# Moving three groups of loads in GpSimd's queue of a fused retention and SwiGLU kernel

## The chip, the cores and the metric

The kernel runs on one core of a Trainium2 chip. The metric is the device time of one execution in microseconds; the time of a kernel is the median of its runs, and lower is better. Where the text says PE, DVE, ACT, POOL and SP it means TensorE, VectorE, ScalarE, GpSimd and SyncE. PEld is the weight load of PE. "POOL's queue" is the in-order list of instructions that GpSimd's sequencer works through; a DMA that is issued from it takes its place among GpSimd's arithmetic.

## What is computed

A retention recurrence over 4 batches, 8 heads, 768 steps of 64 channels, and behind it an RMS norm and a SwiGLU feed-forward layer over the 3072 rows that come out:

```
gamma = 1.0 - 2.0 ** (-5.0 - arange(H))
for t in range(S):
    state = gamma * state + outer(k[:, :, t], v[:, :, t])
    y[:, :, t] = scale * q[:, :, t] @ state
x   = y as (B * S, H * D)
xn  = x / sqrt(mean(x * x) + 1e-6) * rms_g
out = (silu(xn @ w_gate) * (xn @ w_val)) @ w_out
```

All inputs and the output are float32. x has 512 columns, the hidden layer 1536.

## The kernel before

**Tiling.** The 768 steps are cut into six chunks of 128. Inside a chunk the recurrence is done in matrix form: scores q k-transposed under a causal mask with decay, times v, plus q times the state of the chunks before; the state is advanced by k-transposed times v, with v decayed first (`vp`). A chunk has 4 batches. Chunks 0 and 1 take them two at a time, in "pairs" (tiles `q2b`, `k2b`, `v2f`, whose partitions 0 to 63 hold one batch and 64 to 127 the other, two steps to a partition). Chunks 2 to 5 take them one at a time, in "units" (tiles `qb`, `kb`, `v_f`).

**Transposes.** Scores need q and k with channels on partitions. In chunks 0 and 1 PE transposes them (`tp`, L233) and DVE or ACT copies the result out of PSUM. From chunk 2 on the DMA engines transpose them: `t_dma` (L449 to L453) issues two DMA transposes, q first, from SP's queue, each waiting for the load of its source tile. SP's queue also carries the stores of the output (`store`, L545 and L547), and is in order.

**The feed-forward part.** `gv` (L521) makes 128 or 256 columns of the gate product and of the value product on PE (L533), silu on ACT (L537) and their product on DVE (`hT`, L538). `down` (L549) multiplies by w_out (L552), copies out of PSUM on ACT (L554) and stores. The feed-forward part of one chunk is interleaved by hand with the recurrence of the next one, so that PE has work.

**Order.** The program is scheduled by hand: each engine's queue holds its instructions in the order in which the Python code emits them, and nothing moves them afterwards. POOL's queue has both arithmetic and nearly all loads. What stands in it, in order, at the three places that matter here:

- At the start: q and k of pair (0,0) (two DMAs each, one a batch), the iotas `off` and `offp` (L133, L135), q and k of pair (0,1), the iotas `pos_p` and `pos_n` (L139, L141), two small products (L194), four loads of gate and value weights (`load_w`, L86), v of pair (0,1). The two halves of the first v, pair (0,0), are not in it: SP issues them. The first (L119) goes at once; the second (L570) has a dependency, made by hand, on DVE's `late` (L166), so that SP holds it back until then.
- In chunk 0's second half: `power(0, 1)` (L346, the reciprocal root of the mean square), then q, k and v of pair (1,0) (two DMAs each), then `vp_pair(0, 1)` (L276, the decayed v, which `kvp(0, 1)` on PE, L305, waits for), then two loads of weights. Later `vp_pair(1, 0)` reads the v just loaded.
- Between chunk 0's last products and chunk 1's output: `state_diag(1)` (L321), the six loads of units (2,0) and (2,1) (`load`, L105; three DMAs each), `rstd(1, 0)` (L430, then L346), `state_cast(0)` (L324), `vp_pair(1, 1)`, then the six loads of units (2,2) and (2,3). `rstd(1, 0)` waits for ACT's squares of chunk 1's output (L425).

After them SP transposes: `t_dma(2, 0)`, `t_dma(2, 1)`, then the store of `down(0, 3)`, then `t_dma(2, 2)`, `t_dma(2, 3)`. The first PE instructions that need the transposes are `a_pair(2, 0)` (L461, eight matmuls for unit (2,0), eight for unit (2,1)), in step 5 of chunk 1's feed-forward steps; those of units (2,2) and (2,3) are needed by `a_pair(2, 1)` in step 10.

At the start, `v_cast(0)` (ACT, L271) turns v of pair (0,0) to bf16 as `vb`, and `y0(0, 0)` (PE, L291) multiplies by it. `v_cast(1)` does the same for pair (0,1); on ACT it stands ahead of the silu of `gv(0, 2, 3)` and `gv(0, 3, 4)`. `heat` (L215) gives PE matmuls whose result nobody reads.

Of the kernel before, what the change touches and what calls it, by code (L numbers as in the profile page):

```python
# [12 lines left out]
ALU = mybir.AluOpType  # L13
# [3 lines left out]
def kernel(  # L17
# [11 lines left out]
    nc = tc.nc  # L29
# [15 lines left out]
    work = ctx.enter_context(tc.tile_pool(name="work", bufs=4))  # L45
    psum = ctx.enter_context(tc.tile_pool(name="psum", bufs=1, space=bass.MemoryType.PSUM))

    SYNC_DEP = mybir.DependencyInfo(mybir.DependencyClass.Sync, mybir.DependencyReason.DATA)

    srcs = dict(q=q, k=k, v=v)  # L50

    unit_v = {n: s.rearrange("b h (c p) d -> c b p h d", p=C) for n, s in srcs.items()}
# [1 line left out]
    pair_v = {n: s.rearrange("b h (c j e) d -> c b j h (e d)", c=NCH, e=2) for n, s in srcs.items()}  # L54
# [6 lines left out]
    order = [1, 7, 5, 6, 3, 4, 2, 0]  # L61
# [21 lines left out]
    def load_w(n0, n1, *kinds):  # L83
        sl = slice(n0 * 128, n1 * 128)
        for i in kinds or (0, 1):
            nc.gpsimd.dma_start(out=(wg_b, wv_b)[i][:, :, sl], in_=(wg_v, wv_v)[i][:, :, sl])  # L86
# [3 lines left out]

    U = {}

    def load_pair(c, p, n, batches=(0, 1), after=None, eng=None):
        u = U.setdefault((c, p), {})
        if n not in u:
            if n == "v":
                u[n] = work.tile([128, H, 2 * D], F32, name="v2f", bufs=3)
            else:
                u[n] = work.tile([128, H, 2 * D], BF16, name=n + "2b", bufs=4)
        for b in batches:  # L100
            i = (eng or nc.gpsimd).dma_start(out=u[n][b * 64:b * 64 + 64], in_=pair_v[n][c, 2 * p + b])  # L101
            if after is not None:
                tc.add_manual_dep(i.ins, after.ins.name, SYNC_DEP, reason="transfer order")

    def load(c, b, names="qkv"):  # L105
        u = U.setdefault((c, b), {})
        for n in names:
            if n == "v":
                x = work.tile([128, H, D], F32, name="v_f", tag="v_f", bufs=6)
                nc.gpsimd.dma_start(out=x, in_=unit_v[n][c, b])  # L110
            else:
                x = work.tile([128, DM], BF16, name=n + "b", bufs=8)
                nc.gpsimd.dma_start(out=x.rearrange("p (h d) -> p h d", h=H), in_=unit_v[n][c, b])  # L113
            u[n] = x
# [18 lines left out]
    nc.gpsimd.iota(off, pattern=[[1, 128]], base=0, channel_multiplier=-1)  # L133
    for i in range(2):
        nc.gpsimd.iota(offp[i * 64:i * 64 + 64], pattern=[[-1, 2], [1, 2], [2, 64]], base=0, channel_multiplier=-2)  # L135
    load_pair(0, 1, "q")
    load_pair(0, 1, "k")
    for i in range(2):
# [24 lines left out]

    late = const.tile([128, 256], F32, name="late")
    offp_f = offp.rearrange("p e f j -> p (e f j)")
    late_i = nc.vector.tensor_scalar(out=late, in0=offp_f, scalar1=0.0, scalar2=1.0e7, op0=ALU.is_lt, op1=ALU.mult)  # L166
    reach = const.tile([128, 256], F32, name="reach")
    nc.vector.tensor_tensor(out=reach, in0=offp_f, in1=late, op=ALU.add)
    causal_p = const.tile([128, 256], BF16, name="causal_p")
# [84 lines left out]
                        nc.tensor.matmul(ps[i][t, o:o + 128], kt[r, x, b, e], qt[r, x, b], start=True, stop=True)  # L254
        u["a_ps", a] = ps

    last_mask = [None]

    def ap_mask(c, p, a, i):
        u = U[c, p]  # L260
        am = work.tile([128, 2, 2, 128], BF16, name="am2", tag="am", bufs=12)
        m = mask0[a][i] if c == 0 else causal_p[:, None, :].to_broadcast([128, 2, 256])
        last_mask[0] = nc.vector.tensor_tensor(
            out=am.rearrange("p x e t -> p x (e t)"),
            in0=u["a_ps", a][i].rearrange("p (x t) -> p x t", x=2), in1=m, op=ALU.mult)
        u["am", a, i] = am
# [6 lines left out]
    def vp_pair(c, p):  # L273
        u = U[c, p]
        x = work.tile([128, H * 2, D], BF16, name="vp2", bufs=3)
        nc.gpsimd.tensor_tensor(  # L276
            out=x, in0=u["v"].rearrange("p h (e d) -> p (h e) d", e=2),
            in1=vd_p[:, c].rearrange("p h e -> p (h e)")[:, :, None].to_broadcast([128, 2 * H, D]), op=ALU.mult)
        u["vp"] = x.rearrange("p (h e) d -> p h (e d)", e=2)
# [38 lines left out]
    def state_diag(p):  # L318
        for i in range(2):
            r = slice(i * 64, i * 64 + 64)  # L320
            nc.gpsimd.tensor_copy(st_d[p][r, :, :, i * D:i * D + D], st_f[p][r])  # L321

    def state_cast(p):
        nc.gpsimd.tensor_copy(st_b[p], st_f[p])  # L324
# [18 lines left out]
    def power(c, p):  # L343
        u = pair(c, p)
        r = work.tile([128, 2], F32, name="rstd", bufs=4)
        nc.gpsimd.tensor_tensor(out=r, in0=u["ms"], in1=mhalf, op=ALU.pow)  # L346
        u["rstd"] = r
# [11 lines left out]
    def begin(c):  # L359
        XT[c] = work.tile([128, KS, GT], BF16, name="xnT", bufs=2)  # L360
# [18 lines left out]
    def y1(p):  # L379
        u = U[1, p]  # L380
        u["y"] = [bank("y_ps") for _ in range(2)]
        for b in range(2):
            for hp in range(NHP):
                nc.tensor.matmul(u["y"][b][:, hp * 128:(hp + 1) * 128],
                                 u["qT", hp // 2][:, hp % 2, b].rearrange("p e j -> p (e j)"), st_d[p][:, b, hp],
                                 start=hp == 0, stop=False, skip_group_check=True)
        for h in range(H):
            hp, i = h // 2, h % 2
            for e in range(2):
                for b in range(2):  # L390
                    r = slice(b * 64, b * 64 + 64)
                    nc.tensor.matmul(u["y"][b][:, h * D:h * D + D], u["am", hp // 2, i][r, hp % 2, e, :],
                                     u["vp"][r, h, e * D:e * D + D], start=False,
                                     stop=h == H - 1 and e == 1, skip_group_check=True)
# [11 lines left out]
    def pair(c, p):  # L406
        return U[c, p] if c < 2 else U[c, p, "pair"]
# [25 lines left out]
    def norm(c, p, *units):  # L433
        u = pair(c, p)
        if 0 in units:
            u["xn"] = [work.tile([128, DM], BF16, name="xn", bufs=6) for _ in range(2)]
        for b in units:
            nc.vector.scalar_tensor_tensor(out=u["xn"][b], in0=u["x"][:, b], scalar=u["rstd"][:, b:b + 1], in1=g_bc,  # L438
                                           op0=ALU.mult, op1=ALU.mult)
# [81 lines left out]
    def gv(c, n0, n1, t0, t1):  # L521

        if c not in HT:
            HT[c] = work.tile([128, NFF, GT], BF16, name="hT", bufs=1)
        w = t1 - t0
        m = (n1 - n0) * w
        ps = []
        for wt, name in ((wg_b, "g_ps"), (wv_b, "v_ps")):
            x = bank(name, ffn=True)
            for n in range(n0, n1):  # L530
                o = (n - n0) * w
                for s in range(KS):
                    nc.tensor.matmul(x[:, o:o + w], wt[:, s, n * 128:(n + 1) * 128], XT[c][:, s, t0:t1],  # L533
                                     start=s == 0, stop=s == KS - 1)
            ps.append(x)
        sg = work.tile([128, 512], BF16, name="sg", bufs=4)
        nc.scalar.activation(sg[:, :m], ps[0][:, :m], AF.Silu)  # L537
        return nc.vector.tensor_tensor(  # L538
            out=HT[c][:, n0:n1, t0:t1], in0=sg[:, :m].rearrange("p (n t) -> p n t", t=w),
            in1=ps[1][:, :m].rearrange("p (n t) -> p n t", t=w), op=ALU.mult)  # L540
# [8 lines left out]
    def down(c, b):  # L549
        ps = bank("o_ps", ffn=True)  # L550
        for n in range(NFF):
            nc.tensor.matmul(ps, HT[c][:, n, b * C:(b + 1) * C], wo_b[:, n, :], start=n == 0, stop=n == NFF - 1)  # L552
        o_sb = work.tile([128, DM], F32, name="o_sb", bufs=3)
        nc.scalar.copy(o_sb, ps)  # L554
        store(nc.sync, c, b, slice(0, DM), o_sb)
# [11 lines left out]


    begin(0)
    load_pair(0, 0, "v", (1,), after=late_i, eng=nc.sync)  # L570
    load_w(0, 2)
    load_w(2, 4)
    load_pair(0, 1, "v")
# [59 lines left out]
    squares0(1)  # L633
    eps0(1)
    power(0, 1)
    for n in "qkv":
        load_pair(1, 0, n)
    vp_pair(0, 1)
    load_w(10, 12)
    gv(0, 4, 5, 0, 256)  # L640
    gv(0, 5, 6, 0, 256)
# [19 lines left out]
        load_pair(1, 1, n)  # L661
    gv(0, 6, 7, 256, 512)
    state_diag(1)
    load(2, 0)
    gv(0, 7, 8, 0, GT)
    gv(0, 8, 9, 0, GT)
    for n, e in (("q", "a"), ("k", "v")):
# [12 lines left out]
    state1(0)  # L680
    gv(0, 11, 12, 0, GT)
    y1(0)
    load(2, 1)
    down(0, 0)
    y1_out(0)
    square(1, 0, 0)
# [1 line left out]
    rstd(1, 0)  # L688
    state_cast(0)
    norm(1, 0, 0, 1)  # L690
    vp_pair(1, 1)
    load(2, 2)
    down(0, 1)
# [24 lines left out]
    def L(f, *a):  # L718
        return lambda: f(*a)
# [26 lines left out]
    for c in range(2, NCH):  # L746
# [6 lines left out]
        after = {}  # L753
        if d < NCH:
            after = {
                0: [L(begin, d)],
                1: [L(values, d, 0), L(vp, d, 2), L(vp, d, 3)],
                2: [L(y_out, d, 0, 0)] + [L(load, d + 1, 0)] * more,
                3: [L(y_out, d, 0, 1)] + [L(state_add, d, 0)] * more,
                4: [L(square, d, 0, 0)] + [L(load, d + 1, 1)] * more,  # L760
                5: [L(a_pair, d, 1), L(a_mask, d, 2, 0), L(square, d, 0, 1), L(rstd, d, 0)]
                   + [L(state_cast, 0)] * more,
                6: [L(a_mask, d, 2, 1), L(norm, d, 0, 0), L(x_dma, d, 0, 0)]
# [40 lines left out]
```

## Time and profile before

| | |
|---|---|
| median of 5 runs | 241.34 us |
| the five runs | 240.63 to 242.53 us |
| the profiled execution, its own time | 242.53 us |
| the profiled execution, its span | 240.8 us |
| mean granted PE clock in it | 0.989 |
| PE busy | 228.6 us (95%) |
| DVE, ACT, POOL busy | 129.2, 87.4, 116.8 us |
| moved by DMA | 30.24 MB |

The span runs from the first to the last instruction; 1.7 us of the execution's time lie around it. In the views of the profile a line begins with its start in us from the span's start, then how long it took, then the engine, the line of the code and what was written from what; `x2` says that two instructions are merged. Brackets at the end hold the idle time of that engine just before, and after `<-` what ended it. POOLq or SPq lines are DMA issues. The profiled execution is the slowest of the five.

### The profile page before, as it was taken

What the parts mean: (1) busy time and instruction counts of PE and PEld (TensorE: products, weight loads), DVE (VectorE), ACT (ScalarE), POOL (GpSimd) and SP (SyncE); (2) the same over time, 40 slices, a digit from 0 to 9 for tenths busy, and PEclk for the clock granted to TensorE, in tenths of its full rate; (3) what the DMA queues carried; (4) which work ended last, traced back from release to release, by engine and by line L of the source; (5) the groups of instructions that cost most, each with busy time, mean ns of one, the idle gap of its engine ahead of it and who ended that gap; (6) DMA issues with size and microseconds to landing.
All of it is one profiled execution on the core that took longest, in us unless ns stands there. A gap on an engine that the chain in (4) does not pass through costs nothing.

```text
span 240.8 us, 5437 instructions
## 1 busy us (share of the span) xinstructions
PE 228.6 (95%) x2223; PEld 138.7 (58%) x2223; DVE 129.2 (54%) x222; ACT 87.4 (36%) x176; POOL 116.8 (49%) x151
## 2 busy tenths in 40 slices
PE   7689999999996999999999999999999999999993
PEld 2357784545895875585454585454684444854442
DVE  3756734829492687827866336866345842243300
ACT  2576544132342243235223225323225241323220
POOL 8949699789389821990945901927001000000000
PEclk9979999999999999999999999999999999999998
DMA  8999999999999999999699994994520204200022
GB/s 99 170 205 184 170 181 179 188 204 223 148 109 121 183 145 203 126 141 188 52 147 181 121 156 140 99 185 112 143 77 0 44 3 136 82 3 0 0 87 88
DMA packets 82858, 30.24 MB, mean 126 GB/s; under 512 B 69521, under 2 KB 78481, under 8 KB 82834
## 3 DMA queue, kind: packets, MB, share of 16 engines
q0 software_dynamic: 51408, 16.78, 64.7%
q1 hardware_dynamic: 30752, 12.98, 30.4%
q8 instruction: 17, 0.28, 0.5%
q10 hardware_dynamic: 674, 0.14, 0.3%
q14 instruction: 7, 0.06, 0.1%
HBM read 28.32 MB, written 6.29 MB: 144 GB/s over the span
## 4 chain that ended last, share of the span: by engine, by line
PE 77%; DMA 10%; POOL 7%; DVE 3%; issue 1%; ACT 1%; DVEq 0%; POOLq 0%; ACTq 0%
PE o_ps L552 25%; PE g_ps L533 22%; PE v_ps L533 21%; DMA kT<-kb 6%; DMA v2f<-in_v_dram 4%; PE y_ps L506 2%; POOL q2b L101 2%; PE a_ps L461 2%; POOL k2b L101 2%; PE y_ps L490 1%; PE o_ps L563 1%; PE kv_ps L499 1%; POOL v2f L101 1%; PE t_ps L233 1%; POOL vp L276 1%
## 5 line engine op out<-in xcount | busy, mean ns | idle before, releaser
L538 DVE TENSOR_TENSOR hT<-sg,v_ps 128x512 bf16<-128x512 bf16 (+1 forms) x76 | 49.7, 657 | 75.5 <-PE v_ps L533 71.7
L533 PE MATMUL g_ps<-xnT,wg_b 128*128 128x256 bf16 (+1 forms) x428 | 75.0, 310 | 0.2 <-ACT xnT L221 0.2
L533 PE MATMUL v_ps<-xnT,wv_b 128*128 128x256 bf16 (+1 forms) x428 | 74.9, 309 | 0.0
L537 ACT ACTIVATE sg<-g_ps 128x512 bf16<-128x512 f32 (+1 forms) x76 | 43.4, 574 | 82.8 <-PE g_ps L533 82.8
L552 PE MATMUL o_ps<-wo_b,hT 128*128 128x512 bf16 x276 | 61.4, 379 | 0.0
L533 PEld LDWEIGHTS <-wv_b 128*128 128x128 bf16 x428 | 41.8, 98 | 20.8 <-DMA wv_b<-in_moe_w_val_dram 0.2
L533 PEld LDWEIGHTS <-wg_b 128*128 128x128 bf16 x428 | 40.4, 98 | 20.0 <-issue 0.7
L552 PEld LDWEIGHTS <-hT 128*128 128x128 bf16 x276 | 26.5, 98 | 31.4
L430 POOL TENSOR_SCALAR m<-ms 128x2 f32<-128x2 f32 x10 | 2.2, 219 | 69.7 <-ACT xsq L425 69.7
L554 ACT COPY o_sb<-o_ps 128x512 f32<-128x512 f32 x23 | 13.4, 582 | 43.7 <-PE o_ps L552 43.7
L438 DVE SCALAR_TENSOR_TENSOR xn<-x,rstd,g_bc 128x512 bf16<-128x512 f32 x20 | 21.9, 1120 | 12.8 <-POOL rstd L346 12.8
L470 DVE TENSOR_TENSOR am<-a_ps,causal 128x512 bf16<-128x512 f32 x32 | 20.8, 678 | 0.0
L444 POOL TENSOR_TENSOR vp<-v_f,vd_n 128x512 bf16<-128x512 f32 x16 | 20.1, 1277 | 0.0
L425 ACT ACTIVATE xsq<-x 128x512 bf16<-128x512 f32 x20 | 12.4, 623 | 7.7 <-DVE x L416 7.7
L113 POOL DMA_DIRECT2D kb<-in_k_dram x16 | 14.3, 894 | 1.8 <-DMA wo_b<-in_moe_w_out_dram 1.6
L110 POOL DMA_DIRECT2D v_f<-in_v_dram x16 | 14.7, 916 | 0.9 <-DMA qb<-in_q_dram 0.9
L113 POOL DMA_DIRECT2D qb<-in_q_dram x16 | 15.0, 939 | 0.0
L416 DVE TENSOR_TENSOR x<-y_ps,yd_n 128x512 f32<-128x512 f32 x16 | 10.8, 683 | 0.6 <-PE y_ps L506 0.6
L218 PE MATMUL hot<-ones 128*128 128x512 bf16 x25 | 9.6, 513 | 1.4 <-DVE ones L145 1.4
L276 POOL TENSOR_TENSOR vp<-v2f,vd_p 128x1024 bf16<-128x1024 f32 x4 | 8.2, 2042 | 0.1
L461 PE MATMUL a_ps<-qT,kT 64*128 64x128 bf16 x128 | 5.5, 218 | 2.5 <-DMA kT<-kb 2.1
L346 POOL TENSOR_TENSOR rstd<-m,mhalf 128x2 f32<-128x2 f32 x10 | 7.2, 718 | 0.8
(92 smaller groups left out, 158.0 us busy)
## 6 DMA issues: line engine op xcount, KB each, us to landing
v_f<-in_v_dram POOLq DMA_DIRECT2D x16, 256.0 KB, 8.2
out_dram<-o_sb SPq DMA_DIRECT2D x15, 256.0 KB, 2.3
out_dram<-o_sb SPq DMA_DIRECT2D x17, 128.0 KB, 5.6
qb<-in_q_dram POOLq DMA_DIRECT2D x16, 128.0 KB, 8.0
kb<-in_k_dram POOLq DMA_DIRECT2D x16, 128.0 KB, 7.9
wg_b<-in_moe_w_gate_dram POOLq DMA_DIRECT2D x6, 256.0 KB, 6.2
wv_b<-in_moe_w_val_dram POOLq DMA_DIRECT2D x6, 256.0 KB, 6.8
v2f<-in_v_dram POOLq DMA_DIRECT2D x6, 256.0 KB, 9.4
```

Source lines behind the costliest of these rows:

```text
L101: i = (eng or nc.gpsimd).dma_start(out=u[n][b * 64:b * 64 + 64], in_=pair_v[n][c, 2 * p + b])
L110: nc.gpsimd.dma_start(out=x, in_=unit_v[n][c, b])
L113: nc.gpsimd.dma_start(out=x.rearrange("p (h d) -> p h d", h=H), in_=unit_v[n][c, b])
L425: nc.scalar.activation(xsq, u["x"][:, b], AF.Square, scale=1.0 / math.sqrt(DM), accum_out=u["ms_"][:, b:b + 1])
L438: nc.vector.scalar_tensor_tensor(out=u["xn"][b], in0=u["x"][:, b], scalar=u["rstd"][:, b:b + 1], in1=g_bc, op0=ALU.mult, op1=ALU.mult)
L444: nc.gpsimd.tensor_tensor(out=x, in0=U[c, b]["v"], in1=vd_n[:, c, :, None].to_broadcast([128, H, D]), op=ALU.mult)
L470: nc.vector.tensor_tensor(out=x, in0=u["a_ps"][i].rearrange("p (a t) -> p a t", a=NHP), in1=causal[:, None, :].to_broadcast([128, NHP, 128 ...
L533: nc.tensor.matmul(x[:, o:o + w], wt[:, s, n * 128:(n + 1) * 128], XT[c][:, s, t0:t1], start=s == 0, stop=s == KS - 1)
L537: nc.scalar.activation(sg[:, :m], ps[0][:, :m], AF.Silu)
L538: return nc.vector.tensor_tensor(out=HT[c][:, n0:n1, t0:t1], in0=sg[:, :m].rearrange("p (n t) -> p n t", t=w), in1=ps[1][:, :m].rearrange( ...
L552: nc.tensor.matmul(ps, HT[c][:, n, b * C:(b + 1) * C], wo_b[:, n, :], start=n == 0, stop=n == NFF - 1)
L554: nc.scalar.copy(o_sb, ps)
```

## The change

Three things move, all in or into POOL's queue, and the hand-made dependency and the variable that goes with it are taken out.

1. The second half of the first v (batch 1 of pair (0,0)) is issued from POOL, between `offp` and q of pair (0,1), and no longer from SP behind `late`.
2. v of pair (1,0) is issued after `vp_pair(0, 1)` and no longer before it.
3. The six loads of units (2,0) and (2,1) are issued after `rstd(1, 0)`, `state_cast(0)` and `norm(1, 0, 0, 1)` (the last is on DVE), right ahead of `vp_pair(1, 1)`, and no longer ahead of `rstd(1, 0)`.

The arithmetic, the tiles and their buffer counts stay as they are, and so does the order on PE, ACT and DVE.

```
-    def load_pair(c, p, n, batches=(0, 1), after=None, eng=None):
+    def load_pair(c, p, n, batches=(0, 1), eng=None):
...
-            i = (eng or nc.gpsimd).dma_start(out=u[n][b * 64:b * 64 + 64], in_=pair_v[n][c, 2 * p + b])
-            if after is not None:
-                tc.add_manual_dep(i.ins, after.ins.name, SYNC_DEP, reason="transfer order")
+            (eng or nc.gpsimd).dma_start(out=u[n][b * 64:b * 64 + 64], in_=pair_v[n][c, 2 * p + b])
...
         nc.gpsimd.iota(offp[i * 64:i * 64 + 64], pattern=[[-1, 2], [1, 2], [2, 64]], base=0, channel_multiplier=-2)
+    load_pair(0, 0, "v", (1,))
     load_pair(0, 1, "q")
     load_pair(0, 1, "k")
...
     begin(0)
-    load_pair(0, 0, "v", (1,), after=late_i, eng=nc.sync)
     load_w(0, 2)
...
     power(0, 1)
-    for n in "qkv":
+    for n in "qk":
         load_pair(1, 0, n)
     vp_pair(0, 1)
+    load_pair(1, 0, "v")
     load_w(10, 12)
...
     state_diag(1)
-    load(2, 0)
     gv(0, 7, 8, 0, GT)
...
     y1(0)
-    load(2, 1)
     down(0, 0)
...
     norm(1, 0, 0, 1)
+    load(2, 0)
+    load(2, 1)
     vp_pair(1, 1)
     load(2, 2)
```

More of the change, by code (lines that the diff above doesn't have):

```diff
@@ L46 @@
     psum = ctx.enter_context(tc.tile_pool(name="psum", bufs=1, space=bass.MemoryType.PSUM))
-    SYNC_DEP = mybir.DependencyInfo(mybir.DependencyClass.Sync, mybir.DependencyReason.DATA)
     srcs = dict(q=q, k=k, v=v)
@@ L91, with load_pair @@
     U = {}
-    def load_pair(c, p, n, batches=(0, 1), after=None, eng=None):
+    def load_pair(c, p, n, batches=(0, 1), eng=None):
         u = U.setdefault((c, p), {})
@@ L100, in load_pair @@
         for b in batches:
-            i = (eng or nc.gpsimd).dma_start(out=u[n][b * 64:b * 64 + 64], in_=pair_v[n][c, 2 * p + b])
-            if after is not None:
-                tc.add_manual_dep(i.ins, after.ins.name, SYNC_DEP, reason="transfer order")
+            (eng or nc.gpsimd).dma_start(out=u[n][b * 64:b * 64 + 64], in_=pair_v[n][c, 2 * p + b])
     def load(c, b, names="qkv"):
@@ L135 @@
         nc.gpsimd.iota(offp[i * 64:i * 64 + 64], pattern=[[-1, 2], [1, 2], [2, 64]], base=0, channel_multiplier=-2)
+    load_pair(0, 0, "v", (1,))
     load_pair(0, 1, "q")
@@ L165 @@
     offp_f = offp.rearrange("p e f j -> p (e f j)")
-    late_i = nc.vector.tensor_scalar(out=late, in0=offp_f, scalar1=0.0, scalar2=1.0e7, op0=ALU.is_lt, op1=ALU.mult)
+    nc.vector.tensor_scalar(out=late, in0=offp_f, scalar1=0.0, scalar2=1.0e7, op0=ALU.is_lt, op1=ALU.mult)
     reach = const.tile([128, 256], F32, name="reach")
@@ L255, in ap @@
         u["a_ps", a] = ps
-    last_mask = [None]
     def ap_mask(c, p, a, i):
@@ L262, in ap_mask @@
         m = mask0[a][i] if c == 0 else causal_p[:, None, :].to_broadcast([128, 2, 256])
-        last_mask[0] = nc.vector.tensor_tensor(
+        nc.vector.tensor_tensor(
             out=am.rearrange("p x e t -> p x (e t)"),
@@ L569 @@
     begin(0)
-    load_pair(0, 0, "v", (1,), after=late_i, eng=nc.sync)
     load_w(0, 2)
@@ L635 @@
     power(0, 1)
-    for n in "qkv":
+    for n in "qk":
         load_pair(1, 0, n)
     vp_pair(0, 1)
+    load_pair(1, 0, "v")
     load_w(10, 12)
@@ L663 @@
     state_diag(1)
-    load(2, 0)
     gv(0, 7, 8, 0, GT)
@@ L682 @@
     y1(0)
-    load(2, 1)
     down(0, 0)
@@ L690 @@
     norm(1, 0, 0, 1)
+    load(2, 0)
+    load(2, 1)
     vp_pair(1, 1)
```

## The prediction

> **What bounds the kernel now.** I read the page's totals and slices first, then the chain that ended last, then who waited for whom, then the timeline engine by engine round each place that the diff touches.
>
> ```profile
> PE 228.6 (95%) x2223; PEld 138.7 (58%) x2223; DVE 129.2 (54%) x222; ACT 87.4 (36%) x176; POOL 116.8 (49%) x151
> PE   7689999999996999999999999999999999999993
> DMA  8999999999999999999699994994520204200022
> ```
>
> PE is the bound: after the first 30 us (five slices of 6 us) only slice 13 of its row falls under 9. The DMA row is at 9 for nearly all of the first half: loads there queue. So the end can move only through PE's few gaps. The chain and the waits name them:
>
> ```profile
> 12.67 9.78 DMA v2f<-in_v_dram
> 22.53 1.05 ACT vb L271
> ...
> 62.10 13.80 DMA kT<-kb
> 75.95 0.40 PE a_ps L461 x8
> ```
> ```profile
> PE y_ps L291 <- ACT vb L271: 2.0, 2, 1.7
> ...
> PE a_ps L461 <- DMA kT<-kb: 2.1, 1, 2.1
> ...
> PE kv_ps L305 <- POOL vp L276: 0.3, 1, 0.3
> ...
> POOL m L430 <- ACT xsq L425: 5.8, 2, 5.1
> ```
>
> There are three gaps for three edits: 1.7 us at the first y0, 0.3 at kvp(0,1), 2.1 where a_pair(2,0) waits for the fourth DMA transpose, issued at 62.10 and landed at 75.90. The last line matters for edit 3: POOL waits for ACT there, not ACT or DVE for POOL.
>
> **Edit 1, v's second half.** Now:
>
> ```profile
> 6.54 3.30 ACT L180 ACTIVATE mask<-reach,lnscale 128x256 f32<-128x256 f32 x8 [3.22 <-DVE reach L168]
> ...
> 12.01 1.04 ACT L271 CAST vb<-v2f 128x1024 bf16<-128x1024 f32 x1 [2.17 <-DMA v2f<-in_v_dram]
> ```
>
> On POOL it would be issued at 5.24, where q of pair (0,1) begins now, behind k of pair (0,0) in the same queue, which lands at 8.4. The next DMA there took 4.9 us to land, so 10.1 is my estimate; the other end is 12.0, as now. vb then starts up to 1.9 us earlier (ACT is free at 9.84), and y0(0,0), squares, power and x_pe(0,0) follow, up to the first gv, some 1.4 us earlier (the masks end at 11.5, y0 now starts at 13.1). None of it reaches the end: y0(1,0) needs vb of pair (0,1), whose v lands at 22.45, and on ACT the silu of two gv stands behind that cast. So the 1.7 us gap moves from 11.4 to about 22 and keeps its size. When does that v land? Its issue slips by one DMA issue (0.72 us, half of the 1.44 for two at 11.97), but it takes 9.8 us from issue to landing and the DMA share is 1.24 or more in every 5 us from 5 to 25; the same bytes are ahead of it, so the landing stays. I take 0, with 0.72 to either side. Everything else that POOL has in between slips by 0.72 too: pos_n, read by DVE's exponents at 9.69, would be ready at 9.3 instead of 8.6 (cover 0.4; without it the masks slip by the rest). SP loses two issues, and has nothing else before 51 us.
>
> **The clock beside it.** The granted clock is 1.00 from 5 to 10, 0.86 from 10 to 15, 0.80 from 15 to 20 and 1.00 after: 1.7 us of clock lost (0.14 and 0.20 of 5 us), following the 1.7 us gap. If a gap of that size in front of y0(1,0) does it again at 24 us, PE, gapless there, loses up to 1.7. The Trainium skill ("TensorE: Matmul & The Clock Gate", Part 1) has the array fall to half clock after at least one idle window of about 3.4 us; by that rule 1.7 us of idling costs nothing in either place, but the row shows a loss after just such a gap. The other gap of that size, 2.1 us at 73.8, is followed by a clock of 1.00 (the stretches 70 to 75 and 75 to 80), with PE busy nearly without a break ahead of it, as it would be ahead of the new one, while PE was busy 3.71 of the 5 us ahead of the first. I take 0; 1.7 is the bound.
>
> **Edit 2, decayed values first.**
>
> ```profile
> 29.48 1.44 POOL L101 DMA_DIRECT2D v2f<-in_v_dram  x2
> 30.86 1.99 POOL L276 TENSOR_TENSOR vp<-v2f,vd_p 128x1024 bf16<-128x1024 f32 x1
> ```
>
> vp_pair(0,1) starts 1.4 us earlier, ending at 31.4, before kvp(0,1) wants it at 32.6: the 0.31 gap goes. v of pair (1,0) is issued 2.0 later and lands (5.8 and 6.2 after issue now) at 37.3 and 38.5; vp_pair(1,0), at 37.85 now, waits some 0.6. Behind it on POOL are the loads of pair (1,1) and state_diag(1). The first are not needed before t_ps at 55.9, and vp itself ends at 40.4 for kvp(1,0) at 42.8: covered by 2.4. Sum: -0.31, between 0 and -0.31.
>
> **Edit 3, the loads behind the power.**
>
> ```profile
> 45.12 0.91 POOL L113 DMA_DIRECT2D qb<-in_q_dram  x1
> ...
> 51.12 0.92 POOL L110 DMA_DIRECT2D v_f<-in_v_dram  x1
> 52.80 0.22 POOL L430 TENSOR_SCALAR m<-ms 128x2 f32<-128x2 f32 x1 [0.75 <-ACT xsq L425]
> ...
> 54.36 2.34 POOL L276 TENSOR_TENSOR vp<-v2f,vd_p 128x1024 bf16<-128x1024 f32 x1
> 56.65 0.99 POOL L113 DMA_DIRECT2D qb<-in_q_dram  x1
> ```
>
> The power gains nothing: POOL was idle 0.75 us before it. The loads start where vp starts now, 54.36 less the 0.31 = 54.05, 9 us later than now; POOL then idles from 45 to 52.5. Six issues take 5.5 us (0.99, 0.89, 0.91, 0.90, 0.90, 0.94), so vp_pair(1,1) runs from 59.6 to 61.9, against y1(1) at 62.9: covered by 1.0. The loads of (2,2) and (2,3) come 5.3 later (61.9 on, against 56.65). rstd(1,1) slips about 0.6 behind them, and x_pe(1,1) has hardly 0.1 of cover for that: up to 0.3, before a_pair(2,0), whose wait swallows it.
>
> Now SP. It is busy with stores until 57.8 whatever the loads do:
>
> ```profile
> 57.81 1.30 SPq L452 DMA_TRANSPOSE qT<-qb  x1
> 59.21 1.27 SPq L452 DMA_TRANSPOSE kT<-kb  x1
> 60.66 1.34 SPq L452 DMA_TRANSPOSE qT<-qb  x1
> 62.10 1.57 SPq L452 DMA_TRANSPOSE kT<-kb  x1
> ```
>
> The loads now land at 53.7, 55.4, 56.7, 57.6, 58.9 and 59.5 (issue plus 8.6, 7.8, 8.2, 8.2, 8.6, 8.4), behind w_out and pair (1,1). That backlog will have landed at 53.2 (the last v of pair (1,1): 43.2 plus 10.0). In a quiet queue, at 102.7, the first such load took 5.3. So q of (2,0) lands at 59.35, and with today's spacing the three others that SP waits for at 61.05, 63.25 and 64.55: the fourth transpose goes out 2.45 later than 62.10. How long it then takes decides the change. Ten transposes of chunks 2 and 3 show a landing: 8.3, 8.4, 8.5, 8.5, 9.0, 9.4, 11.1, 13.2, 13.4, 13.8. The 13.8 is its own now, when all six loads of (2,2) and (2,3) were issued before it; after, only two and a bit are. kT of (2,0) met loads at that stage, 2.6 us after the first of (2,2), and took 9.4, with one transpose ahead where now three are. I take half the way from it to the ten's mean, 10.4: 9.9. Landing 64.55 + 9.9 = 74.45 against 75.90: **-1.45**, and the -0.31 is in it, since loads follow the power, which follows PE. Ends: no wait left, -2.12 - 0.31 = -2.4; 13.8 again, 78.35, +2.45.
>
> Store of down(0,3) stands behind the four on SP and slips with them; its buffer is next wanted at 90. Next on SP is kT of (2,3): its load, issued at 65.6 for 60.25, took 15.0 (9.6 in unit (3,1)), the transpose 8.5, so it lands between 83.7 and 89.1. PE wants it at 87.4 now, 85.9 in my sum; with 11.1, q's own in that unit, 85.2: covered.
>
> **Sum.** Edit 1: 0. Edits 2 and 3: -1.45. The profiled execution is 242.53 (span 240.8 and 1.7 around it): 241.1 after. It lies 1.2 above the median of 241.34 and no row tells where; I carry the difference over: **239.9**.
>
> **Rivals.**
> - Slower: the loads pile up with the transposes, because the DMA engines get nothing from POOL for some 3 us (53.2 to about 56) in a stretch where their row is full. a_pair(2,0) then waits longer than now. It decides from a latency of 11.35 (no change) and 12.55 (slower by 0.5%); three of the ten rows are above that. At 13.8: 243.8.
> - The wait moves on to a_pair(2,1): at 89.1 that is 1.7 late, 243.0. Against it: 15.0 belongs to the fullest stretch.
> - No change that can be told: latency 10.2 to 12.5, or the clock's loss takes the gain back. PE's loss delays the power and the loads alike: 74.45 + 1.7 is 76.15, 241.6.
>
> **How the numbers follow.** A measurement of this kernel can tell about 0.5% (1.2 us) from no change. Six of ten rows give faster by more than that (latency to 10.15); the second wait and the queue of three ahead take some off: 0.43, my forecast, whose own range is 238.8 to 240.1. Within: 0.22. Slower: 0.25 for the transpose and 0.10 for the second wait and the clock, 0.35. Range: below, the wait gone, 238.8; above, nearly the 13.8 case, 243.4.
>
> **What would show it.** vb of pair (0,0) at about 10, of pair (0,1) still near 22.5; no wait of kvp(0,1); first load of unit (2,0) near 54.0; four transposes at about 59.4 to 64.6, the last landing by 74.5; a_ps L461 waiting less than 1 us. A wait of more than 2 us there, or at the L461 of 85 to 87, a clock below 1.00 near 25 us, or v of pair (0,1) not landing at 22.5 would prove steps wrong.

## The result, and the profile after

The changed kernel takes **246.15 us** (median of 51 runs, 239.68 to 255.17); the kernel before, on the same chips, 240.73 us (93 runs, 239.07 to 244.98). 33 of the 51 runs are above 243.5 us, and 6 of the 93. The ratio of the two is 1.003, with a 95% interval of 1.001 to 1.0051. This ratio, like all ratios below, compares only runs within 1.5% of each kernel's own fastest (of the changed kernel 18 of these 51 and 2 of 6 when it ran again, of edit 3 alone 4 of 12), so for an unsteady kernel the median and the range say more. The changed kernel is slower, and it has become unsteady.

The profiled execution took 250.35 us, its span is 248.6 us, 7.8 above the 240.8 of before. Its page begins:

```profile
PE 230.1 (93%) x2223; PEld 138.6 (56%) x2223; DVE 127.8 (51%) x222; ACT 87.5 (35%) x176; POOL 117.2 (47%) x152
PE   6885999999999799749999999999999999999993
DMA  8999999989999999993099899397440203300022
```

PE's work is the same (2223 matmuls), with more holes: slices 14, 17 and 18 of its row (81 to 87 us, 99 to 112 us) were at 9 before. The DMA row falls to 8 in slice 9 (50 to 56 us), and to 3 and 0 in slices 19 and 20 (112 to 124 us), where it had 9 and 6. Who waits for whom on PE (us in total, times, longest):

```profile
PE g_ps L528 <- DMA xnT<-xn: 5.3, 2, 3.5
PE y_ps L286 <- ACT vb L266: 1.9, 1, 1.9
PE a_ps L456 <- DMA kT<-kb: 1.9, 2, 1.3
PE v_ps L528 <- DMA wv_b<-in_moe_w_val_dram: 1.2, 2, 0.7
```

kvp's 0.3 is gone, the first y0's wait is as long as before in another place, and two waits are new: 5.3 us for xn's DMA transposes and 1.2 us for value weights. The chain that ended last, in order of time (start, length, what):

```profile
13.39 9.80 DMA v2f<-in_v_dram
23.27 1.04 ACT vb L266
...
66.32 8.13 DMA kT<-kb
...
78.58 8.00 DMA kT<-kb
...
99.28 3.56 DMA xnT<-xn
...
104.53 6.82 DMA xnT<-xn
```

Before, the chain had one transpose, kT at 62.10. Now it has four. The second, kT of unit (2,3), is one that the forecast had called covered; for the last two the forecast had no step at all. SP's queue of the changed kernel, and behind it the same place of the kernel before:

```profile
64.77 1.20 SPq L447 DMA_TRANSPOSE qT<-qb  x1
66.32 1.77 SPq L447 DMA_TRANSPOSE kT<-kb  x1
...
97.22 3.28 SPq L511 DMA_TRANSPOSE xnT<-xn  x2
...
103.21 2.61 SPq L511 DMA_TRANSPOSE xnT<-xn  x2
```
```profile
94.04 3.35 SPq L516 DMA_TRANSPOSE xnT<-xn  x2
...
100.10 2.52 SPq L516 DMA_TRANSPOSE xnT<-xn  x2
```

The fourth transpose lands at 66.32 + 8.13 = 74.45. The two last transposes of xn go out 3.1 us later than before, and POOL issues chunk 4's loads from 101.97 on (102.70 before): before, xn's transposes were ahead of those loads and landed 2.4 us after their issue; now they are among them and take 5.8 and 6.8. What PE does there (in brackets the idle time ahead of the instruction), and the stretches behind it (length; busy time and instructions of PE, PEld, DVE, ACT, POOL; granted clock, DMA share, GB/s):

```profile
74.50 0.40 PE L456 MATMUL a_ps<-qT,kT 64*128 64x128 bf16 x8 [0.59 <-DMA kT<-kb]
...
86.62 0.40 PE L456 MATMUL a_ps<-qT,kT 64*128 64x128 bf16 x8 [1.27 <-DMA kT<-kb]
...
102.98 1.03 PE L528 MATMUL g_ps<-xnT,wg_b 128*128 128x256 bf16 x8 [1.80 <-DMA xnT<-xn]
...
111.39 1.89 PE L528 MATMUL g_ps<-xnT,wg_b 128*128 128x256 bf16 x8 [3.48 <-DMA xnT<-xn]
```
```profile
105.00:110.00 5.00, 2.91 (x63) 2.35 (x61) 1.36 (x2) 0.60 (x1) 2.39 (x3) 1.00 1.63 163
110.00:115.00 5.00, 3.60 (x18) 2.55 (x19) 0.00 (x0) 0.60 (x1) 0.00 (x0) 0.51 1.18 247
115.00:120.00 5.00, 5.00 (x28) 3.07 (x27) 3.42 (x6) 1.91 (x4) 0.00 (x0) 0.80 0.00 1
```

Against the profile before: the wait for xnT +5.3, for wv_b +1.2, for the first transposes +0.5, kvp -0.3, kT -0.2, vb -0.1, together +6.4 (PE's idle time in all, span less busy time: 18.5 in place of 12.2). After the 3.48 us gap the clock is 0.51 and then 0.80, by my estimate up to 3.4 us lost in 10 us, where the kernel before lost up to 1.7 at 10 to 20 us and the changed one nothing there: +1.7. Together 8.1, for a span that is 7.8 longer; the clock's part is a little less, since PE was idle in part of these stretches (its busy time grew by 1.5). POOL does nothing from 110 to 120 us, so the next loads start late as well; that is the 3 and the 0 of the DMA row.

### The profile page after: what moved, and what is told of

It is laid out like the page before. It is cut to its first block, busy times and chain, and to the rows that moved or that the text cites. A ratio compares the mean times of both kernels' runs of the same rounds, so it can differ in the third digit from the quotient of the medians.

```text
span 248.6 us, 5435 instructions
## 1 busy us (share of the span) xinstructions
PE 230.1 (93%) x2223; PEld 138.6 (56%) x2223; DVE 127.8 (51%) x222; ACT 87.5 (35%) x176; POOL 117.2 (47%) x152
## 4 chain that ended last, share of the span: by engine, by line
PE 72%; DMA 15%; POOL 5%; DVE 4%; issue 1%; ACT 1%; DVEq 0%; POOLq 0%; ACTq 0%
PE g_ps L528 22%; PE o_ps L547 21%; PE v_ps L528 21%; DMA kT<-kb 6%; DMA xnT<-xn 4%; DMA v2f<-in_v_dram 4%; PE a_ps L456 1%; PE y_ps L501 1%; POOL q2b L99 1%; POOL k2b L99 1%; PE o_ps L558 1%; DVE xn L433 1%; PE y_ps L485 1%; PE t_ps L230 1%; DVE hT L533 1%
## 5 line engine op out<-in xcount | busy, mean ns | idle before, releaser
L528 PE MATMUL g_ps<-xnT,wg_b 128*128 128x256 bf16 (+1 forms) x428 | 76.8, 315 | 5.6 <-DMA xnT<-xn 5.3
L528 PE MATMUL v_ps<-xnT,wv_b 128*128 128x256 bf16 (+1 forms) x428 | 76.1, 313 | 1.2 <-DMA wv_b<-in_moe_w_val_dram 1.2
L528 PEld LDWEIGHTS <-wg_b 128*128 128x128 bf16 x428 | 41.0, 100 | 26.6 <-DMA xnT<-xn 5.9
L433 DVE SCALAR_TENSOR_TENSOR xn<-x,rstd,g_bc 128x512 bf16<-128x512 f32 x20 | 20.5, 1055 | 13.3 <-POOL rstd L341 13.2
L215 PE MATMUL hot<-ones 128*128 128x512 bf16 x25 | 8.2, 449 | 1.4 <-DVE ones L142 1.4
```

## The experiments

Two questions: which of the three edits costs the time, and by what. Each experiment's diff is against the kernel before, unless it says against the changed one. "Here" is the median of the kernel before in the runs beside it, on the same chip.

**Edit 3 alone (only3).** The six loads of units (2,0) and (2,1) behind `rstd(1, 0)`, the rest as before.

```
     state_diag(1)
-    load(2, 0)
...
     y1(0)
-    load(2, 1)
...
     norm(1, 0, 0, 1)
+    load(2, 0)
+    load(2, 1)
     vp_pair(1, 1)
```

> Edit 3 alone (the loads of units (2,0) and (2,1) behind the power). Theory A, a hole in the DMA work: POOL gives the DMA engines nothing from about 45 to 54 us, the loads stand idle for some 4 us in a stretch where they are otherwise full, the backlog ends some 4 us later (near 99 instead of 95 us), and the transposes on SP's queue land late up to chunk 2's xnT. Then this edit alone gives all of the loss: a median between 244 and 250, with runs spread over more than 5 us. Theory B, the start: the loss comes from the first v and its queue; then this kernel stays within 1 us of the one before.

Measured: 245.07 us (241.01 to 250.59, 12 runs), here 240.25; ratio 1.0065 [1.0025, 1.0105]. Nine of the 12 are above 243.5 us, none of the 31 beside them. So the loss and the spread are edit 3's for the greater part. Its profiled execution is the fastest of the 12 (241.01 us): PE's only wait of the new kind is there 0.65 us, for xn's last transpose. What the long runs wait for is seen in the changed kernel's profiles alone.

```profile
105.22 1.03 PE L533 MATMUL g_ps<-xnT,wg_b 128*128 128x256 bf16 x8 [0.65 <-DMA xnT<-xn]
```

**Edit 1 alone (only1).**

```
         nc.gpsimd.iota(offp[i * 64:i * 64 + 64], ...)
+    load_pair(0, 0, "v", (1,))
     load_pair(0, 1, "q")
...
     begin(0)
-    load_pair(0, 0, "v", (1,), after=late_i, eng=nc.sync)
     load_w(0, 2)
```

> Edit 1 alone (the first v's second half from POOL). Theory A: within 1 us of the kernel before, 240 to 242, since vb of pair (0,1) is the wait that ends last in both; at most 0.7 later where its load lands 0.7 later. Theory B: the clock or that late load cost 2 us and more, 243 or above.

Measured: 241.37 us (240.68 to 243.87, 13 runs), here 240.25; ratio 1.0047 [1.0024, 1.0069]. Some 1.1 us slower, and steady. PE's waits in its profile, and the stretch behind the gap at 23 us, where its clock falls to 0.55:

```profile
PE y_ps L292 <- ACT vb L272: 2.7, 2, 2.1
...
PE v_ps L534 <- DMA wv_b<-in_moe_w_val_dram: 1.3, 1, 1.3
```
```profile
25.00:30.00 5.00, 3.72 (x46) 2.29 (x46) 2.30 (x7) 1.50 (x5) 3.63 (x6) 0.55 1.39 177
```

**Edit 2 alone (only2).**

```
-    for n in "qkv":
+    for n in "qk":
         load_pair(1, 0, n)
     vp_pair(0, 1)
+    load_pair(1, 0, "v")
```

> Edit 2 alone (decayed values ahead of v of pair (1,0)). Theory A: 0 to 0.3 us faster than before, 240 to 241.5, and no wait of kvp(0,1) on POOL. Theory B has no price for it either; above 242.5 both are wrong on it.

Measured: 241.07 us (238.59 to 243.01, 12 runs), here 240.25; ratio 1.0008 [0.9975, 1.0042]: no change that can be told. kvp's wait is gone, and a wait of 1.0 us of x_pe (L366) for xn has come in its place. POOL's timeline says why:

```profile
49.68 0.88 POOL L113 DMA_DIRECT2D kb<-in_k_dram  x1 [1.74 <-DMA wo_b<-in_moe_w_out_dram]
...
54.47 0.72 POOL L346 TENSOR_TENSOR rstd<-m,mhalf 128x2 f32<-128x2 f32 x1
```

The loads of chunk 2 are held back until w_out has landed, and the power stands behind them: 54.47, against 53.10 before; of these 1.4 us PE's own progress accounts for 0.4 (kvp(1,0) starts at 43.17, against 42.77), and 1.0 is left, the wait of x_pe. Ahead of such a load seven others are issued and not yet landed; the one that it waits for is the eighth back. So edit 2 pushes the power back, and that is what edit 3 would have been good for.

**Edits 1 and 2 without edit 3 (both12).**

> Edits 1 and 2 without edit 3. Theory A: within 1 us of the kernel before and a spread as narrow as its own (about 4 us at most); the change's loss is gone. Theory B: the loss stays, a median of 244 or more.

Measured: 242.21 us (241.04 to 243.2, 8 runs), here 240.25; ratio 1.0073 [1.0043, 1.0103]. Steady again without edit 3, but 2.0 us above the kernel before, twice what I had allowed and about what the medians of the two alone add up to (1.1 and 0.8): part of the changed kernel's loss may be theirs. Its profile, of its fastest run, has no wait for kT, and 1.6 us of x_pe for xn.

**The kernel before, once more (before_again).**

> The kernel before once more, for a second profile of it. If the 2.1 us wait on kT at a_pair(2,0) belongs to every execution, it is there again. If it belonged to that one execution (242.53 us, 1.8 above the median of many), the wait is absent or under 0.5 us here; then edit 3 had nothing to gain in most executions.

Measured: 240.36 us (239.1 to 241.53, 8 runs), here 240.78; ratio 0.9998. The question was the 2.1 us wait for kT on which the forecast was built. Its waits on PE, behind the 1.4 us of the very first matmuls:

```profile
...
PE t_ps L233 <- DMA q2b<-in_q_dram: 0.7, 1, 0.7
PE y_ps L291 <- ACT vb L271: 0.6, 1, 0.6
PE a_ps L461 <- DVE st_f L512: 0.3, 1, 0.3
PE kv_ps L305 <- POOL vp L276: 0.3, 1, 0.3
```

There is none for kT; nor is there in the profiles of edit 1 alone and of edit 2 alone, which leave the order of SP's and POOL's work at that place as it was. In an ordinary execution there was nothing for edit 3 to win.

### What of edit 3 costs the time

Two theories were left: the loads come too late for what needs them; or the DMA engines stand without loads for some microseconds, and that work is missing at the end of the stretch in which they are full. DMA share and moved bytes from 50 to 55 us in the two edits' extremes:

```profile
50.00:55.00 5.00, 5.00 (x25) 2.29 (x24) 0.33 (x1) 2.40 (x6) 1.31 (x3) 1.00 0.57 122
```
```profile
50.00:55.00 5.00, 5.00 (x25) 2.25 (x23) 0.21 (x2) 2.40 (x6) 4.84 (x8) 1.00 1.83 194
```

The first is edit 3 alone, the second the kernel `swap` below; the kernel before has 1.86 there. Counted from the traces, packets of POOL's loads (those of 128 bytes and more) that start in each microsecond of the span, and their sum:

```
                50   51   52   53   54   55   56   57   58   59    sum
before         136  826  912  254  798 1030  244   72   17  267   4556
swap           228  335  751  682  428  699  768  430  376  925   5622
half3          193  188  791  844  260   80    3  305  843  721   4228
edit 3 alone    74   25    2    0    0    0   18  796  833  363   2111
```

**Swap.** As late for units (2,0) and (2,1) as edit 3, with no hole: the loads of (2,2) and (2,3) take the early places.

```
     state_diag(1)
-    load(2, 0)
+    load(2, 2)
...
-    load(2, 1)
+    load(2, 3)
...
     norm(1, 0, 0, 1)
+    load(2, 0)
+    load(2, 1)
     vp_pair(1, 1)
-    load(2, 2)
...
-    load(2, 3)
     t_dma(2, 1)
```

> The kernel before, with the loads of units (2,2) and (2,3) at the early place (before rstd(1,0)) and those of units (2,0) and (2,1) behind the power, as late as in edit 3. There is no hole in the DMA work, but the units that are transposed first land as late as in the changed kernel. Theory A, the hole's backlog: 239.8 to 241.5. Theory L, lateness of the first two units: as edit 3 alone, 244 or more, spread over 5 us and more.

Measured: 239.93 us (238.97 to 241.98, 12 runs), here 241.03; ratio 0.9967 [0.9937, 0.9996]. Not slower and steady, with the loads of units (2,0) and (2,1) just as late. So the lateness of these two units is not the cause; the hole stands, and with it the lateness of all loads behind it, which this run does not tell apart from it.

**Half of edit 3 (half3).** Only unit (2,1)'s three loads go behind the power.

```
     y1(0)
-    load(2, 1)
...
     norm(1, 0, 0, 1)
+    load(2, 1)
     vp_pair(1, 1)
```

> The kernel before, with unit (2,1)'s three loads alone moved behind the power; unit (2,0)'s stay ahead. The hole in the DMA work is about half as long (loads start at 45, stop at 49, go on at 54). Theory A, the hole's length sets the backlog: between the two, a median of 241 to 243.5. If only the position of unit (2,0)'s transposes on SP counted: as before, 240 to 241.

Measured: 240.31 us (239.25 to 243.77, 12 runs), here 240.58; ratio 0.9978 [0.9951, 1.0006]. I had expected a loss, and there is none. The count shows a hole of some two microseconds at 55, but the kernel before has one like it at 57, and over the ten microseconds both move about the same (4228 and 4556 packets); edit 3 alone moves half. The short hole is moved, not added.

**Where the missing work comes due: late4 and xfirst**, both against the changed kernel. late4 moves chunk 4's first six loads behind the power of unit group (3,0), out of the way of xn's transposes; xfirst lets xn's transposes pass those of chunk 3's units (3,2) and (3,3) on SP.

```
-                2: [L(y_out, d, 0, 0)] + [L(load, d + 1, 0)] * more,
+                2: [L(y_out, d, 0, 0)] + [L(load, d + 1, 0)] * (more and c > 2),
...
-                   + [L(state_cast, 0)] * more,
+                   + [L(load, d + 1, 0), L(load, d + 1, 1)] * (c == 2) + [L(state_cast, 0)] * more,
```

> The changed kernel, with the first six loads of chunk 4 moved behind the power of chunk 3's first half (rstd(3,0)), so that they start some 10 us later. Theory A1: in the changed kernel SP's transposes of chunk 2's xn go out 3 us later than before and so meet the data of chunk 4's loads; that meeting (6.8 us to land in place of 2.4) is the larger part of the loss. Then PE's waits on xnT in chunk 2's first steps shrink to under 1.5 us in all, and the median falls from 246 to 242.5 or less. Theory A2: lateness alone, the transposes of xn stand in SP's in-order queue behind q and k transposes that wait for late loads; then the xnT waits stay and the median stays at 244 or more.

```
-        11: [..., L(t_dma, 3, 2)],
-        12: [L(values, 2, 1), ..., L(x_dma, 2, 0, 1), L(t_dma, 3, 3),
+        11: [...],
+        12: [L(values, 2, 1), ..., L(x_dma, 2, 0, 1),
...
-             L(rstd, 2, 1), ..., L(x_dma, 2, 1, 1),
+             L(rstd, 2, 1), ..., L(x_dma, 2, 1, 1), L(t_dma, 3, 2), L(t_dma, 3, 3),
```

> The changed kernel, with the four transposes of units (3,2) and (3,3) moved behind the four of chunk 2's xn in SP's queue. A1 and A2 both: xn's transposes go out when DVE has made xn, no longer behind transposes that wait for late loads; no wait on xnT over 1 us, median 242.5 or less. A3, the loss is in the waits on kT at 75 and 87 us: median stays at 244 or more.

Measured, late4: 249.13 us (247.4 to 249.99, 6 runs), ratio 1.0347 [1.0295, 1.0399]; xfirst: 243.45 us (241.6 to 244.41, 6 runs), ratio 1.012 [1.0066, 1.0175]; here 240.58. late4 as a remedy is a miss. PE's wait for xnT is gone as expected, though xn's last transposes go out at 102.64 and 103.95, only 0.6 us earlier than in the changed kernel: without chunk 4's loads beside them they land after 2.4 us. But chunk 4's transposes are late now, and one wait has become 4 us:

```profile
136.51 0.61 PE L456 MATMUL a_ps<-qT,kT 64*128 64x128 bf16 x8 [3.97 <-DMA kT<-kb]
```

xfirst has 0.9 us of wait for xnT left, as expected, and none of its six runs reaches the changed kernel's median; its own median lies between the limits of the two theories. It is 2.9 us above the kernel before, edits 1 and 2 without edit 3 are 2.0 above it, the changed kernel 5.4. So the long runs come in good part from xn's transposes going out among chunk 4's loads; how the spread divides over the waits, and why some executions pay 0.65 us and others several, is open.

**The changed kernel, once more (after_again).**

> The changed kernel once more, beside the kernel before on the same chip. Theory A: a median of 243 to 249 and runs more than 5 us apart; PE waits on transposes that land late (kT at 75 or 87 us, xnT at 100 to 112 us), in amounts that differ from the first profile.

Measured: 249.13 us (242.95 to 253.99, 6 runs), here 241.03; ratio 1.0136 [1.0062, 1.0209]. The spread is there again, and the median is at the upper end of what was expected. Its profile is of a shorter execution (span 243.9) and has the two largest waits again, the first one smaller:

```profile
PE g_ps L528 <- DMA xnT<-xn: 3.7, 2, 2.0
PE y_ps L286 <- ACT vb L266: 2.2, 1, 2.2
```

**Transposes earlier (early_t).** `t_dma(2, 0)` ahead of the stores of `down(0, 1)` and `down(0, 2)`, as another way to end the wait for kT.

```
     load(2, 2)
+    t_dma(2, 0)
     down(0, 1)
     down(0, 2)
-    t_dma(2, 0)
```

> The kernel before, with the two transposes of unit (2,0) moved ahead of the stores of down(0,1) and down(0,2) in SP's queue: their loads land at 53.7 and 55.4, and SP issues them only at 57.8 now. If the last kT's landing at a_pair(2,0) is bound by work queued on the DMA engines, its wait (2.1 us in the profile of before) shrinks by 1 to 2 us, and the kernel is 0.5 to 1.5 us faster, 239 to 240. If that wait is bound by the loads of units (2,2) and (2,3) beside it, nothing changes.

Measured: 240.48 us (239.14 to 241.22, 12 runs), here 240.58; ratio 1.0 [0.9978, 1.0022]. No gain, which fits a wait that is mostly not there.

### What of edit 1 costs the time

Its profile shows two things: a lower clock from 25 to 30 us, and a wait for weights.

**only1_heat** adds ten of `heat`'s matmuls, whose result nobody reads, ahead of `y0(1, 0)`, so that PE has no long gap there.

```
     gv(0, 3, 4, 0, 256)
+    heat(10, 2)
     y0(1, 0)
```

> Edit 1 alone with ten idle-filling matmuls (heat) put on PE between gv(0,3,4) and y0(1,0), where edit 1 leaves PE without work for about 2 us. Theory C, the clock: edit 1 costs its 1.1 us (241.4 against 240.25) because that gap lets the granted clock fall at 25 to 30 us in part of the runs (0.55 and 0.66 in three profiles of five with edit 1, 1.00 in all five without). Then the fillers bring the clock in that stretch to 1.00 and the median to 240.6 or less. Theory D, transfers: edit 1 delays loads in POOL's queue; then the median stays at 241.2 or more.

Measured: 241.38 us (240.24 to 247.32, 12 runs), here 240.78; ratio 1.0033 [1.0004, 1.0063]. In its profile the clock from 25 to 30 us is 1.00, and the kernel is still slower; the wait for wv_b is 1.2 us, about as without heat (1.3). So the lower clock is not the whole cause; whether it is a part can't be told, since this interval and that of edit 1 alone overlap.

**vfirst1**: edit 1, and v of pair (0,1) ahead of `load_w(2, 4)`.

> Edit 1 with v of pair (0,1) issued ahead of load_w(2, 4). If y0(1,0) is bound by the landing of that v in both kernels, as the prediction said, the landing comes some 2 us sooner, the gap closes from the other side, and edit 1's 1.4 us at the start reach the end: 238.8 to 239.8, clock 1.00 at 25 us. If the weights of load_w(2, 4) then bind, PE waits for wv_b by 1 us and more and nothing is gained.

Measured: 241.24 us (239.48 to 243.37, 12 runs), here 240.78; ratio 1.0015 [0.9981, 1.005]. v comes sooner (vb at 20.79) and weights later (waits of 1.7 for wg_b and 0.8 for wv_b): a wait is exchanged for another.

**v_sp_now**: the second half is issued at once, as early as can be, but from SP.

```
-    load_pair(0, 0, "v", (0,), eng=nc.sync)
+    load_pair(0, 0, "v", (0, 1), eng=nc.sync)
...
-    load_pair(0, 0, "v", (1,), after=late_i, eng=nc.sync)
```

> The kernel before, with the first v's second half issued by SP at once, without the wait for DVE's late, so on SP's ring and not on POOL's. Theory D1, the ring: edit 1 costs because 256 KB more stand in POOL's ring, and the weights of load_w(4, 6) behind them land near 25.7 in place of 24.1 us; here POOL's ring is as before, so no wait of PE on wv_b near 25 us and a median of 239.8 to 240.8. Theory D2, earliness itself (an early vb leaves PE a gap, the clock falls, or the early DMA holds up q and k of pair (0,0)): 241.2 or more, as edit 1.

Measured: 240.88 us (238.9 to 243.26, 12 runs), here 241.03; ratio 0.9981 [0.995, 1.0013]; with edit 1 alone it was 1.0047 [1.0024, 1.0069]. vb of pair (0,0) starts at 9.77, as early as edit 1 makes it, and there is no wait for wv_b. The instructions that issue the value weights in question, first here, then with edit 1 and heat (two loads in that window), each with the times from issue to landing:

```profile
L86 POOL DMA_DIRECT2D wv_b<-in_moe_w_val_dram x1: 765/765/765, 17.7 to 17.7; - x1
...
DMA to landing us min/median/max: 6.3/6.3/6.3
```
```profile
L86 POOL DMA_DIRECT2D wv_b<-in_moe_w_val_dram x2: 745/754/762, 16.0 to 17.8; - x2
...
DMA to landing us min/median/max: 11.0/11.1/11.3
```

With the half on SP these weights land at 17.7 + 6.3 = 24.0, with the half in POOL's queue (the first of the two loads) at 16.0 + 11.0 = 27.0, though they were issued 1.7 us earlier. The same reading gives 24.6 and 23.9 for the two profiles of before, 26.3 for edit 1 alone and 25.5 for the changed kernel; there PE waits for the weights ahead of these, which land at 18.05 and 20.95 in place of 16.25 and 19.12. Over all traces it is 23.7 to 25.1 in the ten with the half on SP and 24.1 to 27.0 in the eight with it in POOL's queue. The two overlap: in both12 (24.1) and in the changed kernel's second profile (24.4) the weights are not late and PE does not wait for them. In the kernel before and in v_sp_now the half is on SP, at different times, and the weights land alike; so not its time but its queue is what costs. That it costs by way of these weights fits the profiles, but not every execution shows it.

### A version that beats both

**e2_half3**: edit 2, and only unit (2,1)'s loads behind the power; edit 1 left out. **e2_half3_early** has early_t's move as well.

```
-    for n in "qkv":
+    for n in "qk":
         load_pair(1, 0, n)
     vp_pair(0, 1)
+    load_pair(1, 0, "v")
...
     y1(0)
-    load(2, 1)
...
     norm(1, 0, 0, 1)
+    load(2, 1)
     vp_pair(1, 1)
```

> Edit 2, with unit (2,1)'s three loads alone behind the power. In edit 2 alone the power came 1.3 us late (rstd at 54.5 in place of 53.1) because the loads ahead of it waited for w_out to land, and PE waited 1.0 us for xn. If that coupling is what eats edit 2's 0.3, this kernel has no such wait and gives 239.7 to 240.4; if edit 2's gain is lost elsewhere, 240.6 or more.

> Edit 2, unit (2,1)'s loads behind the power, and unit (2,0)'s transposes ahead of two stores. e2_half3 gave 239.46 beside 240.78; the transposes' place was worth nothing alone. Expected as e2_half3: 0.2 to 0.6% below the kernel before.

Measured: e2_half3 **239.46 us** (238.41 to 242.03, 12 runs), here 240.78, ratio 0.9965 [0.9937, 0.9992]; e2_half3_early 240.25 (239.33 to 241.72, 12 runs), here 241.03, ratio 0.9956 [0.9931, 0.9982]. POOL's timeline of e2_half3:

```profile
48.81 0.88 POOL L113 DMA_DIRECT2D kb<-in_k_dram  x1 [1.68 <-DMA wo_b<-in_moe_w_out_dram]
49.69 0.89 POOL L110 DMA_DIRECT2D v_f<-in_v_dram  x1
52.19 0.22 POOL L430 TENSOR_SCALAR m<-ms 128x2 f32<-128x2 f32 x1 [1.60 <-ACT xsq L425]
52.49 0.72 POOL L346 TENSOR_TENSOR rstd<-m,mhalf 128x2 f32<-128x2 f32 x1
```

The loads still wait for w_out, but only three are ahead of the power, and it is back at 52.49 with 1.6 us to spare. Both kernels gain about 0.4%, and so does swap (0.3%); the three can't be told apart.

## Why the prediction was wrong

The forecast of 239.9 us failed in sign, and 246.15 lies above the range's 243.4. By its steps:

- **"PE's few gaps": the 2.1 us wait for kT.** The gain of 1.45 in the sum was read from one execution that was 1.2 us above the median, and I wrote that "no row tells where" these 1.2 us were. The second profile of the same kernel has no such wait and a span of 237.6. What edit 3 can win in an ordinary execution is near 0, not 1.45.
- **Edit 3, the path of kT.** Loads from 54.05 (55.06 measured), `vp_pair(1, 1)` 59.6 to 61.9 (60.4 to 62.4), the fourth transpose at 64.55 and landed at 74.45 (66.32 and 74.45, its latency 8.1 and not 9.9: two misses that cancel, by luck). a_pair waits 0.59. This part held.
- **Edit 3, what is late next: the step that failed.** I followed the delayed stream to the first consumer and gave the next as "covered" (85.2 against 85.9). kT of (2,3) landed at 86.58, within the 83.7 to 89.1 that I had given, and PE waited 1.27 for it, which was the second rival. Behind that I looked at nothing. But the hole was not made good before the loads ran out: by the packets in the traces chunk 3's last loads end at 89.9 to 94.9 us in the thirteen profiles without edit 3 (half of it and swap included), and at 97.0 to 99.7 in the four of the changed kernel and its variants late4 and xfirst; edit 3 alone, in its fastest run, ends at 94.9, within the first range. In the changed kernel kT of (2,3) goes out at 78.58 in place of 75.28, when its load has landed; the transposes of chunk 3 and of xn stand behind it in the same in-order queue on SP, and PE waits 1.8 us for xn's second transpose, which is late with them. A delay of 3 us carries xn's last two into the loads of chunk 4, and there PE waits 3.5 us more.
- **The rival "slower"** named the mechanism ("the DMA engines get nothing from POOL for some 3 us") and looked for its price in the same wrong place, the latency of one transpose. The hole was five microseconds long, not three: from 52 on hardly a packet of the backlog starts (24 in the four microseconds to 56), not from 53.2, and the new loads' packets begin at 57, not 56. The price was paid 30 to 55 us later.
- **Edit 1 at 0, ends ±0.72: mis-sized.** It costs about 1.1 us by itself (1.0047 [1.0024, 1.0069]). vb(0,0) at 9.90, the gap's move to 22 and its size (1.9) were right, and v of pair (0,1) landed 0.74 later, about the bound that I gave. The argument for 0, "the same bytes are ahead of it", failed for the weights, which land later in six of the eight profiles with edit 1: bytes that SP's queue had carried beside POOL's now stand in front of them. The loss of clock, taken as 0 with a bound of 1.7, came in some executions: in only1 0.55 from 25 to 30 us and 0.77 from 30 to 35, up to 3.4 us by my estimate, twice the bound; in the changed kernel none there.
- **Edit 2, -0.31.** kvp's wait went as computed. I covered the delayed v up to `vp_pair(1, 0)` and did not ask what the two moved loads do to the next issues on POOL: the loads of chunk 2 wait longer for w_out and hold the power up by 1.0 us.
- **"The power gains nothing"** held for the kernel before, not with edit 2 in it: the three edits do not add up one by one, and e2_half3 uses just this.

## What to carry to other kernels

Where the DMA engines are full, moving loads behind a wait can leave them with nothing to move for some microseconds, and here that was paid at the end of the full stretch, by what stood there: follow the backlog to the first pause and not to the first consumer. Swapping which loads go early kept the queue fed and cost nothing. A wait read in one execution is worth its mean over executions, and an execution above the median by about the size of the wait should be taken as a warning. Bytes moved to another engine's queue can delay what stands behind them there.

## What the runs showed of the hardware

- **The issuing queue matters when the queues are full.** The Trainium skill ("DMA: Bandwidth & Descriptors", Issuing engines are not separate DMA queues) says that DMAs issued from several engines run on the same 16 DMA engines and that issuing from more of them saves only the sequencer's time. Here 256 KB on SP instead of POOL left the time as it was (v_sp_now, 0.9981 [0.995, 1.0013]), and on POOL they cost (only1, 1.0047 [1.0024, 1.0069]); the weights behind them in POOL's queue landed at 24.0 and 26.3 us in these two. Why is open: that the DMA engines move less in all is not shown, since from 6 to 16 us they moved 1.53 to 1.76 MB in the eight profiles with the half in POOL's queue and 1.63 to 1.77 in the ten without.
- **The clock can fall after gaps shorter than the page's window.** "TensorE: Matmul & The Clock Gate", Part 1, has half clock after an idle window of about 3.4 us. The 3.48 us gap at 108 us agrees (0.51 after it). But in the kernel before the clock was 0.86 from 10 to 15 us and 0.80 from 15 to 20, with a gap of 1.7 us at 11, and in edit 1 alone a gap of 2.1 us and one of 1.3 gave 0.55; in both12 a gap of 2.1 alone left it at 1.00.
- **A DMA transpose beside loads takes a multiple of its own time.** xn's last two: 2.4 us each ahead of chunk 4's loads (the kernel before) or without them (late4), 5.8 and 6.8 among them (the changed kernel).
- **POOL holds a load back while eight earlier ones are in flight**, as every wait of that kind in only2 and e2_half3 has it (0.45 to 1.74 us); a load in the queue can so delay arithmetic behind it. Whether the chip or the compiled program does the holding is not told apart.
